# Small VectorE operations on SBUF made on GpSimd and ScalarE, a planner that knows the shared SBUF port, and TensorE listed in two lanes

## The chip, the cores and the metric

The kernel runs on one core of a Trainium2 chip. Its engines work from queues of their own and wait for one another by semaphores: TensorE (PE, with its weight loads PEld) multiplies matrices into PSUM, VectorE (DVE) and ScalarE (ACT) compute on SBUF and PSUM, GpSimd (POOL) computes on SBUF, and SyncE (SP) issues nearly all DMA transfers. The metric is the device time of one execution in microseconds (us), lower is better; the time of a kernel is the median of its runs.

## The reference

```python
def reference(A_x, A_wqkv, A_wo, B_x, B_w1, B_w3, B_w2):
    x = A_x                                   # (1, 2048, 512)
    xn = _layernorm(x, axis=-1)
    s = _A_ref(xn, A_wqkv, A_wo)              # attention, 32 heads of 16, causal, window 256
    g = _silu(_B_ref(xn, B_w1, B_w3, B_w2))   # (silu(xn w1) * (xn w3)) w2, inner width 1792
    return x + s * g
```

All inputs and the output are float32.

## The kernel before

**Tiles.** The 2048 tokens are cut into four token tiles t of 512, the 32 heads into four groups g of eight, and each group into two halves p. A (t, g, p) is a unit of attention; there are 32, and they run in this order. The kernel keeps float32 accuracy on 16-bit matmuls: every factor is scaled by a power of two and split into a high and a low float16 half, and a product is three matmuls (high by high, high by low, low by high).

**Attention.** For a unit, `pass1` multiplies queries by keys into a scores bank of PSUM (`s`, or `po` in a batch marked X), and VectorE takes each query's masked maximum into `M` (L616). When all eight rows are there, L621 and L622 split the negated maxima into two float16 halves `NM`; TensorE transposes them in the next unit (`finish`, L631), VectorE copies them out (L637) and SyncE sends them through DRAM into two extra rows of the queries `qa`. The extra rows of the keys `KA` hold constant ones, so that `pass2` gets scores with the maximum already subtracted: matmuls with the keys standing (L678), the mask added by VectorE (L685), the exponential by ScalarE (L688), then the product with the values V (L706), whose last column of ones gives the denominator. `normalise` inverts the denominators (L743, with a scale in L744) and multiplies.

**Feed-forward.** For a tile t and a block f of 128 columns, `gate_up` makes two products of 24 matmuls (L937); ScalarE takes the tanh (L948), VectorE the two products (L952, L957), and the result is split by ScalarE and GpSimd (L963, L316). `down` (first tile, and the last blocks of the last tile) multiplies with w2 (L987) and VectorE adds the bank to its sum (L1007); for the other tiles `product` does the same with seven products of half blocks instead of eight (L1040, L1053), whose left and right factors GpSimd sums (L869 to L872, L910 to L913).

**What is special in the first tile.** During t = 0 the weights arrive as float32. Each is measured: sums of squares (`squares`), added over partitions by TensorE beside a row of scores (`powers`, L279), then turned on VectorE into a power of two and its inverse on 128x1 to 128x6 elements (L288 to L294) and into scales (L798 to L800, L849 to L855). With these ScalarE and GpSimd split the weights (L319, L320, L316), and SyncE stores them for the later tiles. The inverse root of layernorm is a chain of twelve steps on 128x4 elements on VectorE (`rstd`, L427 to L437), once for each tile; the centred tokens (L440) are turned by TensorE beside scores (`turn_beside`, L478) and split by two VectorE operations, L487 (high half) and L488 (low half). The tiles 1 and 2 are prepared within t = 0, tile 3 within t = 1.

**What sets the order.** The program is written down as one list: a unit's batches of scores, between them (`spread`) the dense pieces of the feed-forward and projections. TensorE runs it in that order. Matmuls of dense pieces go into two banks `m0` and `m1` by turns, so a new dense bank waits until the one before last has been emptied. The other engines are ordered by `listed`: it plays the list through, with a cost for each instruction (`cost`) and a delay to its reader (`extra`), and takes on each engine, among the instructions that are ready, the one that is due first; due times (`deadlines`) are counted back from TensorE's own clock. In its costs a VectorE operation on four elements takes 84 ns, whatever GpSimd does. The order found is fixed by dependencies without semaphores.

## Time and profile before

| | us |
|---|---|
| median of 3 runs (lowest, highest) | 819.23 (818.41, 819.41) |
| profiled execution, its own time | 821.13 |
| its span, first to last instruction | 819.3 |
| ScalarE busy | 435.3 |
| mean granted TensorE clock | 0.994 |
| VectorE's groups L621 and L622, 32 each | 9.0 and 9.7 |
| VectorE's group L744, 16 | 4.4 |

A row of the profile names the line, the engine, the operation, the tile written and the tiles read, the shapes and the count. After the bar stand the busy us of the group and the mean ns of one, then the engine's idle time just before, and what ended it. In a timeline the first number is the start in us, the second the length; brackets hold the idle time before and what ended it. A busy TensorE is not TensorE at its peak: the ends of matmuls are modelled. The granted clock is 1.00 at full speed.

### The profile page before, as it was taken

How to read it: one execution, taken by the hardware profiler on the slowest of the kernel's cores; microseconds unless marked ns; L12 is line 12 of the kernel's file. 1: busy time of each engine (PE TensorE's matmuls, PEld its weight loads, DVE VectorE, ACT ScalarE, POOL GpSimd, SP SyncE). 2: the span in 40 equal slices, each digit the busy share in tenths (PEclk: the TensorE clock that was granted, in tenths of full speed). 3: DMA queues.
4: the chain of work that ended last, by engine and by line, in shares of the span. 5: the costliest groups of instructions: out<-in, count | busy, mean ns of one | idle time of the engine just before them, and what ended most of it. 6: DMA issues, size and time to landing. Idle time of an engine off the chain costs nothing.

```text
span 819.3 us, 23768 instructions
## 1 busy us (share of the span) xinstructions
PE 797.9 (97%) x9088; PEld 415.8 (51%) x9088; DVE 639.2 (78%) x2044; ACT 435.3 (53%) x659; POOL 358.7 (44%) x556
## 2 busy tenths in 40 slices
PE   8999999699999999999999999999999999999998
PEld 4444444344544554454555555545555555545654
DVE  8898889977897777799778866777878787774535
ACT  6898799555636554443443455534443446544421
POOL 2247646672806433523341752514141456435252
PEclk9999999899999999999999999999999999999999
DMA  9996575268665334545364452426375543224521
GB/s 284 284 296 185 164 215 169 75 197 204 176 179 136 117 103 121 152 144 154 106 189 133 125 142 69 140 72 172 112 185 152 159 146 113 56 90 149 172 65 55
DMA packets 112835, 121.99 MB, mean 149 GB/s; under 512 B 18448, under 2 KB 77008, under 8 KB 112720
## 3 DMA queue, kind: packets, MB, share of 16 engines
q1 hardware_dynamic: 112432, 119.94, 51.2%
q8 instruction: 71, 1.16, 0.6%
q10 hardware_dynamic: 288, 0.52, 0.2%
q14 instruction: 44, 0.36, 0.1%
HBM read 83.76 MB, written 32.37 MB: 142 GB/s over the span
## 4 chain that ended last, share of the span: by engine, by line
PE 83%; DVE 12%; issue 2%; DMA 1%; ACT 1%; DVEq 0%; SPq 0%; ACTq 0%
PE m L937 32%; PE m L1040 9%; PE m L550 9%; PE po L706 8%; PE s L678 5%; PE m L1118 5%; PE m L520 5%; PE m L987 4%; DVE junk L616 3%; PE s L604 3%; DVE s L685 2%; PE po L604 2%; DVE st L422 1%; DMA qa<-dQ 1%; DVE slot L957 1%
## 5 line engine op out<-in xcount | busy, mean ns | idle before, releaser
L688 ACT ACTIVATE pt<-s,es 128x1024 f32<-128x1024 f32 x152 | 167.7, 1113 | 198.0 <-DVE s L685 193.3
L937 PE MATMUL m<-XH,slot 128*128 128x512 f16 x896 | 267.4, 380 | 1.0 <-DVE slot L952 0.8
L316 POOL TENSOR_TENSOR slot<-slot,slot 128x256 f16<-128x256 f32 (+1 forms) x222 | 148.6, 696 | 152.4 <-ACT slot L320 66.6
L937 PEld LDWEIGHTS <-slot 128*128 128x128 f16 x1344 | 124.5, 98 | 152.6 <-issue 12.3
L937 PE MATMUL m<-XL,slot 128*128 128x512 f16 x448 | 169.8, 379 | 0.0
L685 DVE TENSOR_TENSOR s<-s,MK 128x256 f32<-128x256 f32 (+2 forms) x280 | 120.7, 437 | 50.4 <-PE s L678 41.9
L616 DVE CUSTOM_DVE_ANT_0 junk<-s,MW 128x320 bf16<-128x320 f32 x276 | 134.5, 487 | 28.0 <-PE s L604 18.6
L906 POOL TENSOR_TENSOR slot<-slot,slot 128x256 f16<-128x256 f32 x133 | 87.9, 685 | 46.4 <-ACT slot L902 46.3
L1040 PE MATMUL m<-slot,slot 128*128 128x256 f16 x798 | 96.4, 276 | 2.0 <-DVE s L685 1.8
L616 DVE CUSTOM_DVE_ANT_0 junk<-po,MW 128x320 bf16<-128x320 f32 x172 | 84.0, 488 | 10.0
L1040 PEld LDWEIGHTS <-slot 128*128 128x128 f16 x798 | 76.9, 99 | 20.4 <-issue 4.5
L706 PE MATMUL po<-pt,V 64*32 64x320 f32 (+4 forms) x2880 | 78.2, 345 | 0.0
L706 PEld LDWEIGHTS po<-pt,V 64*32 64x32 f32 x2880 | 51.9, 106 | 23.8 <-PE s L604 4.0
L910 POOL TENSOR_TENSOR slot<-slot,slot 128x256 f32<-128x256 f32 x19 | 14.2, 747 | 102.8 <-DVE slot L957 96.5
L678 PE MATMUL s<-qa,KA 50*64 50x320 f16 (+3 forms) x1472 | 58.2, 259 | 1.0 <-ACT pt L688 1.0
L987 PE MATMUL m<-slot,slot 128*128 128x512 f16 x216 | 51.6, 386 | 7.0 <-DVE slot L1007 4.7
L952 DVE SCALAR_TENSOR_TENSOR slot<-slot,m 128x512 f32<-128x512 f32 x56 | 38.3, 683 | 24.0 <-ACT slot L948 23.8
L678 PEld LDWEIGHTS <-KA 50*64 50x64 f16 x1472 | 30.2, 105 | 50.9 <-issue 36.3
L716 ACT COPY os<-po 128x512 f32<-128x512 f32 x32 | 18.7, 585 | 70.2 <-PE po L706 70.2
L948 ACT ACTIVATE slot<-m,sgs 128x512 f32<-128x512 f32 x56 | 38.3, 684 | 32.2 <-PE m L937 31.3
L957 DVE SCALAR_TENSOR_TENSOR slot<-m,slot 128x512 f32<-128x512 f32 x56 | 38.5, 687 | 15.9 <-PE m L937 15.5
L604 PE MATMUL s<-KA,qa 48*64 48x320 f16 (+2 forms) x648 | 45.5, 295 | 1.9 <-DVE M L616 0.7
(170 smaller groups left out, 1137.1 us busy)
## 6 DMA issues: line engine op xcount, KB each, us to landing
slot<-dW SPq DMA_DIRECT2D x88, 256.0 KB
slot<-dR SPq DMA_DIRECT2D x56, 256.0 KB
slot<-in_B_w_dram SPq DMA_DIRECT2D x42, 256.0 KB
dW<-slot SPq DMA_DIRECT2D x32, 256.0 KB
slot<-in_A_x_dram SPq DMA_DIRECT2D x30, 256.0 KB
KA<-dK SPq DMA_DIRECT2D x24, 288.0 KB
dR<-slot SPq DMA_DIRECT2D x49, 128.0 KB
qa<-dQ SPq DMA_DIRECT2D x32, 192.0 KB
```

The costliest lines, as they stand in the source:

```text
L316: op(out[:, c], a[:, c], b[:, c])
L550: nc.tensor.matmul(cell["pp"], a[:, k, c, :], b[:, c, :], start=(c, i) == parts[0][0], stop=(c, i) == parts[-1][-1])
L604: nc.tensor.matmul(s[64 * c:64 * c + 64, r, :n], qa[rows, 2 * p + a, ii * P + 64 * c:ii * P + 64 * c + 64], ka[rows, 2 * p + a, e - n:e], ...
L616: nc.vector.tensor_tensor_reduce(out=junk[:, :n], in0=s[:, r, :n], in1=mask, scale=1.0, scalar=NEG, op0=ALU.add, op1=ALU.max, accum_out=M[ ...
L678: nc.tensor.matmul(s[64 * h:64 * h + 64, r, o:o + 64 * n], ka[rows, 2 * p + a, 64 * (m + 4):64 * (m + 5)], qa[rows, 2 * p + a, 64 * (m + k ...
L685: nc.vector.tensor_add(v, v, MK[:, kind, of:of + n, :].unsqueeze(1).to_broadcast([P, 2 * len(which), n, 64]))
L688: nc.scalar.activation(pt, s, AF.Exp, scale=es)
L706: nc.tensor.matmul(cell["po"][32 * i:32 * i + 32, h, 64 * (m + k):64 * (m + k + n)], V[64 * h:64 * h + 64, (4 * t + m // 2) % VB, hd * VW: ...
L906: nc.gpsimd.tensor_sub(made[:, D + c.start:D + c.stop], raw[:, c], made[:, c])
L937: nc.tensor.matmul(cell[k], w[:, (a * NC + c) * P:(a * NC + c + 1) * P], b[:, c, :], start=c == 0 and i == 0, stop=c == NC - 1 and i == 2)
L987: nc.tensor.matmul(ps, hh[:, a * TW + b * P:a * TW + (b + 1) * P], w[:, c * D:(c + 1) * D], start=f == f0 and i == 0, stop=f == f1 - 1 and ...
L1040: nc.tensor.matmul(ps[:, blk, :], l[:, a * D + q:a * D + q + 128], r[:, 256 * c:256 * c + 256], start=f == f0 and x == 0, stop=f == f1 - 2 ...
```

## The change

It has four parts.

1. *Operations moved.* The roots of tiles 1 to 3 (`rstd_beside`), the powers of two with their inverses, and the scales made from them go to GpSimd once the opening is over (`aside`); the inverse is now an integer subtraction of exponents instead of a reciprocal. The maxima are taken with a scale of 1/ONE and without the sign, which is put into the ones of the keys instead, so that their split is one ScalarE copy and one GpSimd subtraction. The high half of a turn is copied by ScalarE (L487's copy). The scale of the denominators (L744) is dropped: it is in the values' column of ones, which ScalarE now writes. The shift that makes a power of two now reads PSUM.
2. *The planner's costs.* New costs per engine, with terms for operands in SBUF and for a second input; delays by engine, and one between dependent instructions of the same engine; `shares` names the instructions that use the port which VectorE and GpSimd share, and such instructions are played one after the other.
3. *TensorE in two lanes.* The matmuls are cut into blocks of up to six that are dense (bank `m`) or not. Each lane keeps its own order, but where the next block in the list is not ready, the other lane's next may go first, if it is at most 8 us ahead. The play is run four times, each time from the order found before.
4. *Order fixed for TensorE too*, by the same dependencies, and the kernel is no longer traced under a fixed TensorE schedule.

```diff
-                    nc.vector.scalar_tensor_tensor(al, s[:, 1, WIN:WIN + n], 2.08, al, op0=ALU.mult, op1=ALU.add)
-            nc.vector.tensor_scalar(p2, al, 2.0**63, None, op0=ALU.mult)
-            nc.vector.reciprocal(inv, p2)
+                    nc.vector.scalar_tensor_tensor(s[:, 1, WIN:WIN + n], s[:, 1, WIN:WIN + n], 2.08, al, op0=ALU.mult, op1=ALU.add)
+            op = nc.vector if s is None else nc.gpsimd
+            nc.vector.tensor_scalar(al.bitcast(I32), (al if s is None else s[:, 1, WIN:WIN + n]).bitcast(I32), 24, 23,
+                                    op0=ALU.logical_shift_right, op1=ALU.logical_shift_left)
+            op.tensor_scalar(p2, al, 2.0**63, None, op0=ALU.mult)
+            if s is None:
+                nc.vector.reciprocal(inv, p2)
+            else:
+                op.tensor_scalar(inv.bitcast(I32), p2.bitcast(I32), -1.0, float(254 << 23), op0=ALU.mult, op1=ALU.add)
...
+    def aside():
+        return nc.gpsimd if started else nc.vector
...
+        def rstd_beside(b0, b1):
+            op = nc.gpsimd
+            ve = lnpool.tile([P, b1 - b0], F32, name="ve")
+            op.tensor_scalar(ve, mv[:, b0:b1, 1], 1e-5, None, op0=ALU.add)
+            r0 = lnpool.tile([P, b1 - b0], F32, name="r0")
+            op.tensor_scalar(r0.bitcast(I32), ve.bitcast(I32), -0.5, float(0x5F3759DF), op0=ALU.mult, op1=ALU.add)
+            sq = lnpool.tile([P, b1 - b0], F32, name="sq")
+            for i in range(3):
+                op.tensor_mul(sq, r0, r0)
+                op.tensor_mul(sq, sq, ve)
+                op.tensor_scalar(sq, sq, -0.5, 1.5, op0=ALU.mult, op1=ALU.add)
+                op.tensor_mul(r0, r0, sq)
+            op.tensor_scalar(rs[:, b0:b1], r0, XS, None, op0=ALU.mult)
...
-                    nc.vector.tensor_copy(hi, pt)
+                    nc.scalar.copy(hi, pt)
                     nc.vector.tensor_sub(lo, pt, hi)
...
-                nc.vector.tensor_scalar(nm[:, 0, :], Mf, -1.0 / ONE, None, op0=ALU.mult)
-                nc.vector.scalar_tensor_tensor(nm[:, 1, :], Mf, -1.0 / ONE, nm[:, 0, :], op0=ALU.mult, op1=ALU.subtract)
+                nc.scalar.copy(nm[:, 0, :], Mf)
+                nc.gpsimd.tensor_sub(nm[:, 1, :], Mf, nm[:, 0, :])
...
             nc.vector.reciprocal(dr, dr)
-            nc.vector.tensor_scalar(dr, dr, sc["o"], None, op0=ALU.mult)
...
-            nc.vector.tensor_scalar(pi, pi, WS, None, op0=ALU.mult)
-            nc.vector.tensor_scalar(sg_scale[:, ff], pp[:, 0, :], 0.5 / (WS * XS), None, op0=ALU.mult)
-            nc.vector.tensor_mul(p13[:, ff], pp[:, 0, :], pp[:, 1, :])
+            aside().tensor_scalar(pi, pi, WS, None, op0=ALU.mult)
+            aside().tensor_scalar(sg_scale[:, ff], pp[:, 0, :], 0.5 / (WS * XS), None, op0=ALU.mult)
+            aside().tensor_mul(p13[:, ff], pp[:, 0, :], pp[:, 1, :])
...
         if i.engine == ENGINE.Activation:
-            return 130 + 0.98 * n + 50 * (len(i.outs) > 1)
+            return 30 + (0 if psum else 30) + 0.9 * n + 95 * scales + 30 * more
         if i.engine == ENGINE.DVE:
-            return 80 + 1.05 * n + (6 * n if kind == "InstReciprocal" else 0) + 45 * (len(i.outs) > 1)
-        return 40 + 2.6 * n
+            return max(160, (185 if inputs > 1 or len(i.outs[0].ap) < 2 or i.outs[0].ap[-1][1] < n else 95) + 0.98 * n + 55 * (scales == 1) + (5 * n if kind == "InstReciprocal" else 0)) - 80
+        if n <= 64:
+            return 130 + (14 if kind == "InstTensorScalarPtr" else 2.1) * n
+        return 2.68 * n - 42 if inputs else 0.85 * n
+
+    def shares(i):
+        if i.engine == ENGINE.Pool:
+            return type(i).__name__ != "InstMemset"
...
+        if len(big) > 1:
+            return sum(big) > 1
+        return all(big) and getattr(i.outs[0].bass_ap.tensor, "space", None) != PSUM
...
+        def next_block():
+            able = sorted((lane[h] for lane, h in zip(lanes, heads) if h < len(lane)), key=lambda b: when_of[b])
...
+            f = free[ENGINE.PE]
+            first = met[able[0]] if not open_[able[0]] else None
+            if len(able) > 1 and (first is None or first > f + GAIN):
+                o = able[1]
+                if not open_[o] and when_of[o] - when_of[able[0]] < LEADING and (
+                        first is None or max(f, met[o]) + GAIN < first):
+                    return max(f, met[o]), o
+            return None if first is None else (max(f, first), able[0])
...
             start[k] = s
-            free[e] = s + took[k]
+            if shared[k]:
+                s = max(s, port - 140)
+                port = s + took[k] + 80
...
-ROUNDS, SHIFT = 3, False
+PIECE, GAIN, LEADING, FOLLOW = 6, 300, 8000, 0.0
+ROUNDS = 4
```

**VectorE, where the down products of the second group of blocks empty their first bank** (tile 0; `mv`, `rs`, `ve`, `r`, `sq` belong to the root of tile 2, `dsc` is the scale of the sum, `m_2573` the bank). Before:

```order
L427 TENSOR_SCALAR ve<-mv 128x4
L430 TENSOR_SCALAR r_2849<-ve 128x4
L431 TENSOR_SCALAR r_2849<-r_2849 128x4
L434 TENSOR_TENSOR sq<-r_2849 128x4
L435 SCALAR_TENSOR_TENSOR sq<-sq,ve 128x4
L436 SCALAR_TENSOR_TENSOR r_2849<-sq,r_2849 128x4
L437 TENSOR_SCALAR rs<-r_2849 128x4
L440 TENSOR_SCALAR slot_2469<-slot_2469,mv,rs 128x512
L440 TENSOR_SCALAR slot_2471<-slot_2471,mv,rs 128x512
L1007 SCALAR_TENSOR_TENSOR slot_1423<-m_2573,dsc,slot_1423 128x512
```

(L434 to L436 stand there three times.) And now (line 1035 is the old 1007, 510 the old 488, 638 the old 616, 430 and 431 the statistics):

```order
L638 ISA junk,M<-po,MW 128x320
L638 ISA M 128x1
L510 TENSOR_TENSOR XL<-po,XH 128x2x128
L510 TENSOR_TENSOR XL<-s,XH 128x2x128
L431 BN_AGGR mv<-st 128x2
L1035 SCALAR_TENSOR_TENSOR slot_1413<-m_2565,dsc,slot_1413 128x512
L430 BN_STATS st<-slot_2465 128x6
L431 BN_AGGR mv<-st 128x2
L430 BN_STATS st<-slot_2467 128x6
```

The root and the centring no longer stand ahead of the sum that empties the bank; part of that tile's statistics now comes behind it.

**GpSimd, a root among the splits of weights** (tile 0, the root of tile 1; L324 is the old L316, L900 a sum of down weights). These rows were not there; the splits were next to each other:

```order
L436 TENSOR_SCALAR ve<-mv 128x4
L900 TENSOR_TENSOR slot_1576<-slot_816,slot_1575 128x256
L438 TENSOR_SCALAR r_1960<-ve 128x4
L827 TENSOR_TENSOR p_155<-pp 128x2
L441 TENSOR_TENSOR sq<-r_1960 128x4
L442 TENSOR_TENSOR sq<-sq,ve 128x4
L443 TENSOR_SCALAR sq<-sq 128x4
L444 TENSOR_TENSOR r_1960<-r_1960,sq 128x4
L324 TENSOR_TENSOR slot_1327<-slot_806,slot_1327 128x256
L441 TENSOR_TENSOR sq<-r_1960 128x4
L324 TENSOR_TENSOR slot_1327<-slot_806,slot_1327 128x256
```

Root steps and splits now take turns on GpSimd.

**TensorE, the first bank of those down products** (`slot_2428` and `slot_2459` are down weights, `slot_2072` and `slot_2267` the split hidden blocks). Before, the third six of the bank follow the second:

```order
L987 LDWEIGHTS slot_2072
L987 MATMUL m_2573<-slot_2428,slot_2072 128x512
L987 LDWEIGHTS slot_2267
L987 MATMUL m_2573<-slot_2459,slot_2267 128x512
L987 LDWEIGHTS slot_2267
```

And now a batch of scores, with two halves of a turn, comes between:

```order
L1015 LDWEIGHTS slot_2064
L1015 MATMUL m_2565<-slot_2420,slot_2064 128x512
L700 LDWEIGHTS KA_139
L700 MATMUL s<-qa,KA_139 64x320
L700 LDWEIGHTS KA_139
```

There are some eight such places, all but one in the first tile (in the one later place six matmuls of L937 move between two halves of a row of scores); the rest of TensorE's list is as it was.

At the start, five matmuls that only keep TensorE busy (L1327) now stand ahead of the sum of squares of the first weights (L274) instead of behind it; VectorE's powers of two for these weights are worked in between the steps of the first root, and ScalarE casts the weights ahead of the four copies of the turned tokens instead of between them.

191 lines of the change are left out of this document (137 added, 54 removed).

## The prediction

> **What bounds the kernel now.** I read the page first, then the busy time of each engine by stretches, then TensorE's own waits, then the timeline of the one long wait.
>
> ```profile
> span 819.3 us, 23768 instructions
> PE 797.9 (97%) x9088; PEld 415.8 (51%) x9088; DVE 639.2 (78%) x2044; ACT 435.3 (53%) x659; POOL 358.7 (44%) x556
> ```
>
> TensorE sets the time: it is idle for 819.3 - 797.9 = 21.4 us, and the change leaves its 9088 matmuls as they are. Whatever the change wins must come out of those 21.4 us, or out of time at half clock. The stretches show where they lie (columns after the length: busy us and instructions of each engine, then granted clock).
>
> ```profile
> core 0: us, PE busy (x) PEld busy (x) DVE busy (x) ACT busy (x) POOL busy (x), PEclk, DMA share, GB/s
> 60.00:85.00 25.00, 24.20 (x250) 11.25 (x252) 21.53 (x80) 22.37 (x41) 19.69 (x30) 1.00 0.60 181
> 85.00:110.00 25.00, 23.23 (x246) 10.99 (x239) 23.11 (x83) 19.20 (x34) 13.94 (x22) 1.00 0.67 201
> 110.00:135.00 25.00, 24.69 (x308) 12.05 (x305) 20.82 (x87) 23.28 (x43) 9.95 (x16) 1.00 0.62 181
> 135.00:165.00 30.00, 22.96 (x250) 10.60 (x248) 27.90 (x81) 19.22 (x33) 22.32 (x35) 0.89 0.33 99
> 165.00:400.00 235.00, 233.48 (x2773) 119.14 (x2773) 189.45 (x621) 118.44 (x165) 104.04 (x155) 1.00 0.55 153
> 400.00:745.00 345.00, 344.49 (x4315) 186.99 (x4314) 269.06 (x830) 161.23 (x216) 141.56 (x209) 1.00 0.44 126
> 745.00:755.00 10.00, 8.21 (x56) 4.79 (x55) 3.71 (x8) 4.54 (x6) 5.72 (x9) 0.83 0.64 192
> 755.00:819.30 64.30, 60.59 (x574) 34.37 (x571) 32.92 (x66) 17.26 (x23) 22.96 (x32) 1.00 0.33 100
> ```
>
> From 165 to 745 us TensorE idles 1.52 + 0.51 = 2.0 us out of 580: nothing to win there, only something to lose. From 60 to 165 it idles 0.80 + 1.77 + 0.31 + 7.04 = 9.9 us, and in the last of these stretches the clock is 0.89 while VectorE is busy for 27.9 of 30 us. So the change has to act on the first token tile, where the weights are measured and split. TensorE's waits, longest first (us in total, times, longest):
>
> ```profile
> PE m L987 <- DVE slot L1007: 4.7, 1, 4.7
> PE m L987 <- POOL slot L316: 2.0, 5, 0.6
> PE m L1040 <- DVE s L685: 1.8, 1, 1.8
> PE s L678 <- ACT pt L688: 1.0, 1, 1.0
> PE m L937 <- DVE slot L952: 0.8, 2, 0.5
> PE m L520 <- DVE slot L563: 0.8, 1, 0.8
> PE s L604 <- DVE M L616: 0.7, 1, 0.7
> PE s L604 <- ACT pt L688: 0.4, 1, 0.4
> PEld L1040 <- DMA slot<-dR: 2.1, 1, 2.1
> ```
>
> **The long wait and its cause.** The timeline around it, with the same instruction 62 us earlier:
>
> ```profile
> 89.32 0.16 DVE L436 SCALAR_TENSOR_TENSOR r<-sq,r 128x4 f32<-128x4 f32 x1
> 91.23 1.44 POOL L316 TENSOR_TENSOR slot<-slot,slot 128x256 f16<-128x256 f32 x2 [2.77 <-ACT slot L320]
> 149.74 1.46 PE L987 MATMUL m<-slot,slot 128*128 128x512 f16 x6
> 150.70 3.17 POOL L316 TENSOR_TENSOR slot<-slot,slot 128x256 f16<-128x256 f32 x5
> 151.42 0.59 DVE L436 SCALAR_TENSOR_TENSOR r<-sq,r 128x4 f32<-128x4 f32 x1
> 155.05 0.75 DVE L1007 SCALAR_TENSOR_TENSOR slot<-m,dsc,slot 128x512 f32<-128x512 f32 x1
> 155.85 2.72 PE L987 MATMUL m<-slot,slot 128*128 128x512 f16 x6 [4.66 <-DVE slot L1007]
> ```
>
> At 89.32 GpSimd has been idle (it starts again at 91.23, after 2.77 us) and a root step on 128x4 elements takes 0.16 us. At 151.42 GpSimd runs without a break and the same step takes 0.59, nearly one GpSimd operation. The VectorE operations whose operands all lie in SBUF wait for GpSimd; the root of the third tile, which nobody needs yet, stands ahead of L1007, and TensorE waits 4.66 us for L1007 to empty its bank. Then six matmuls take 2.72 us where they took 1.46: 1.26 us of half clock.
>
> The Trainium skill, SBUF — State Buffer, section Who interferes with whom, says that a VectorE instruction with two SBUF inputs, or in a two-port mode, and a GpSimd instruction lock each other out of a shared port for a whole instruction. The pair 0.16 and 0.59 agrees.
>
> **Term 1: the root and the small scales leave VectorE.** In 135 to 165 us:
>
> ```profile
> L436 DVE SCALAR_TENSOR_TENSOR r<-sq,r 128x4 f32<-128x4 f32 x3 | 1.8, 612 | 0.1
> L435 DVE SCALAR_TENSOR_TENSOR sq<-sq,ve 128x4 f32<-128x4 f32 x3 | 1.8, 588 | 0.1
> L434 DVE TENSOR_TENSOR sq<-r 128x4 f32<-128x4 f32 x3 | 1.4, 469 | 0.1
> L487 DVE CAST XH<-po 128x256 f16<-128x256 f32 x3 | 1.3, 420 | 0.0
> ```
>
> These four groups alone are 6.3 of VectorE's 27.9 us and all go. In the new VectorE list no root step stands ahead of the bank's release; four statistics and two halves of a turn do, and a whole block of 18 matmuls covers them (six take 1.46 us with the last one's tail, so 18 take some 4). I count the wait and its clock as gone: 4.66 + 1.26 = 5.9 us. If half the cover were missing, 3 us would be left.
>
> **Term 2: the smaller waits of the same kind**, L952 0.8, L616 0.7 and L688 1.0 + 0.4 (its mask add waits on VectorE): 2.9 us. They follow other roots and powers of two on VectorE. I take 2.3, between 0 and 2.9.
>
> **Term 3: after 165 us.** L563's 0.8 stands behind maxima, not behind a root, but VectorE loses work there too. I take 0.4, with 2.0 (all idle time) as the bound. L1040's wait is no VectorE wait: the weight load of the same product waits 2.1 us for a DMA of dR, whose slot and place in SyncE's list stay nearly as they were. I leave it, half clock (0.83) included.
>
> **Term 4: what GpSimd gets.** No row of before has a GpSimd operation on so few elements. The bounds and the rows nearest in size:
>
> ```profile
> L316 POOL TENSOR_TENSOR slot<-slot,slot 128x256 f16<-128x256 f32 x156 | 101.3, 678 | 102.8 <-ACT slot L320 66.6 <-ACT slot L963 33.5 <-ACT slot L877 1.6
> L221 POOL TENSOR_SCALAR_AFFINE_SELECT MK<-MK 64x64 bf16<-64x64 bf16 x4 | 0.8, 234 | 0.0
> L227 POOL MEMSET NM<- 128x64 f16 x3 | 0.4, 152 | 0.0
> L902 ACT CAST slot<-slot 128x256 f16<-128x256 f32 x19 | 7.6, 402 | 5.2 <-DVE slot L957 5.2
> ```
>
> A memset of 64 columns takes 0.15, a select of 64 columns 0.23, a two-input operation on 256 columns 0.68. One to sixteen columns lie nearest the 64: I take 0.23 each, between 0.15 and 0.68. Of 132 moved operations 27 fall into 135 to 165 us (15 of the root, two measurements of 5, two maxima): 27 x 0.23 = 6.2 us on top of 22.3, in a stretch that shrinks from 30 to 24 us. GpSimd is then over-full by 4.5 us there. Part can slide: the sums of the down weights and the normalising products are not urgent, and TensorE's list now has a scores batch and two turns between the second and the third six of the down matmuls that waited 2.0 us for L316. I take 0.9 us lost, between -2.0 (those waits gone) and +4.5.
>
> **Term 5: ScalarE's share.** 24 halves of a turn at about 0.40 (the 128x256 cast) are 9.6 us, 32 copies of maxima at 0.2 to 0.4 some 10, on an engine 53% busy. Each first half was followed by its second on VectorE; now that waits for ScalarE, behind an exponential at worst, while the scores bank stays held. The maxima chain gets one engine longer. The tightest place is the last unit:
>
> ```profile
> 741.51 0.18 DVE L622 SCALAR_TENSOR_TENSOR NM<-M,NM 128x16 f16<-128x16 f32 x1
> 742.79 0.22 PE L631 MATMUL s<-identh,NM 64*64 64x64 f16 x2
> ```
>
> 742.79 - 741.69 = 1.1 us of slack, enough for one more hand-over when ScalarE and GpSimd are free. I take 0.2 lost, between 0 and 3.
>
> **Term 6: the start.**
>
> ```profile
> 9.68 0.17 DVE L437 TENSOR_SCALAR rs<-r 128x4 f32<-128x4 f32 x1
> 9.98 0.19 PE L274 MATMUL s<-sb,onesb 128*128 128x1 bf16 x2 [1.53 <-DVE sb L259]
> 14.88 1.02 PE L550 MATMUL s<-XH,whi 128*128 128x512 f16 x4 [0.46 <-ACT XH L459]
> ```
>
> The first tile's root stays on VectorE, but the first weights' scale is now worked in between its steps, and one of those steps waits for L274, which now stands behind five more warm-up matmuls. The root's end at 9.85 slips to about 11; the first projection hangs on the last ScalarE copy, and ScalarE now casts the weights ahead of those copies instead of between them. Between -0.3 and +1.2; I take 0.4.
>
> **The sum.** -5.9 - 2.3 - 0.4 + 0.9 + 0.2 + 0.4 = -7.1 us. The profiled execution took 821.13 us (span 819.3 and 1.8 around it), so 814.0 for such a one; the median of the runs, 819.23, lies 1.9 below it, which gives **812.1 us**.
>
> **Rivals.**
>
> *All waits go.* If term 4 falls on its good side and the new lists also catch the rest, the waits listed above but L1040's (4.7 + 2.0 + 1.0 + 0.8 + 0.8 + 0.7 + 0.4 = 10.4) and the clock's 1.26 vanish: 807.5. For it: the planner's new costs and second lane move work away from exactly these places. Against it: GpSimd's load.
>
> *GpSimd becomes the bound* in the first tile. At 0.68 us for each small operation, 27 cost 18.4 us and the stretch needs 22.3 + 18.4 = 40.7 us: 10.7 more than before, less terms 2 and 3: 827. The point from which it decides is (30 - 22.3)/27 = 0.29 us an operation, where the stretch is as long as it was. The select's 0.23 speaks against it, the dependence of each root step on the one before for it.
>
> *Nothing is won.* The lock is only turned round: where VectorE waited for GpSimd, the small steps now queue on GpSimd behind 0.68 us each, and their consumers (weight splits, maxima) are late instead. If half of term 1 and all of terms 2 and 3 come back as waits for GpSimd, 3.0 us are left of the gain; 2.0 us of new waits after 165 us and 0.3 at the start leave 0.7: 818.5. Against it: the maxima and mask adds that fill VectorE (L616, L685) have a scores bank, not SBUF, as their large input, so they do not wait for GpSimd now and need not then.
> The Trainium skill, Perfetto Trace Analysis, section Optimizing Scalar/DVE Operations, warns that moving operations between GpSimd and VectorE "might not help", since they share an SBUF read port. By that rule this rival is the outcome.
>
> *Scores banks held longer.* 24 turns and 32 maxima with 0.1 us each passed on to TensorE would cost 5.6 us; with half of the 7.1 lost too that is 821.3. The slack of units before the last speaks against it.
>
> **How the numbers follow.** Forecast 0.54 (809 to 816); all waits go 0.20; nothing won 0.13; GpSimd the bound 0.08; banks 0.05. The range to the other cases is 805 to 820. A measurement of this kernel tells 0.2%, 1.6 us, from no change. Faster by more: 0.54 + 0.20 + 0.05 of the third case = 0.79. Within: 0.08. Slower: 0.13.
>
> **What would show it.** Right: no wait on L1035 (the old L1007) of over 1 us and no half clock near 150 us; root steps on GpSimd at 0.2 to 0.3 us; VectorE under 600 us busy, its remaining small steps at 0.16; TensorE's idle time near 14 us, still with a DMA wait near 740 us. Wrong: small GpSimd steps of 0.5 us or more, TensorE waiting for L316's successor in several pieces between 130 and 165 us, or new waits between 165 and 745 us that sum to more than 3 us, where before has 2.0.

## The result, and the profile after

| | us |
|---|---|
| before, median of 10 runs (lowest, highest) | 819.72 (818.41, 821.44) |
| after, median of 10 runs (lowest, highest) | 816.24 (814.42, 818.09) |
| ratio, 95% interval | 0.9954 (0.9941 to 0.9967) |
| profiled execution of after, its own time and span | 818.09, 816.3 |

The change won 3.5 us where 7.1 were forecast: faster by more than 0.2%, by half of the size. The ten executions of after differ by 3.7 us, and the mean granted clock of TensorE goes with them: 0.993 at 818.1 us, 0.998 at 814.4 to 815.3. The profiled execution is the slowest of the ten, 1.9 us above the median, and so holds more half clock than most. In the changed kernel the old L1007 is L1035, L316 is L324, L987 is L1015, L688 is L710, L440 is L462, L1093 is L1121, L1118 is L1146 and L1040 is L1068. The page of after begins:

```profile
span 816.3 us, 23767 instructions
PE 798.9 (98%) x9088; PEld 417.8 (51%) x9088; DVE 591.5 (72%) x1846; ACT 445.6 (55%) x716; POOL 382.7 (47%) x678
```

VectorE lost 47.7 us of work, ScalarE got 10.3 and GpSimd 24.0. TensorE idles 17.4 us (816.3 - 798.9) instead of 21.4. Its busy time by stretches, with the columns shown before:

```profile
60.00:135.00 75.00, 73.81 (x803) 35.00 (x802) 54.90 (x203) 65.45 (x123) 54.97 (x118) 1.00 0.69 211
135.00:165.00 30.00, 28.18 (x340) 14.02 (x338) 20.15 (x70) 23.85 (x45) 27.87 (x54) 1.00 0.36 107
...
755.00:816.30 61.30, 54.50 (x480) 29.40 (x457) 26.77 (x52) 13.98 (x19) 20.63 (x30) 0.96 0.26 79
```

From 60 to 135 us TensorE now idles 1.2 us (before, in three stretches, 2.9), from 135 to 165 us 1.8 (before 7.0), and the clock there is 1.00 (before 0.89). From 165 to 745 us it idles 4.1 us instead of 2.0, but 2.1 of these are the old wait for a DMA of dR, which in after comes at about 741 to 743 us and so ahead of 745. Behind 755 us it idles 6.8 us where it idled 3.7, at a clock of 0.96 instead of 1.00. Its longest waits in after:

```profile
PE m L1146 <- DVE slot L1035: 3.0, 1, 3.0
PE m L478 <- DVE slot L462: 2.1, 1, 2.1
PE m L1068 <- DMA slot<-dR: 2.1, 1, 2.1
...
PE m L1015 <- POOL slot L324: 0.5, 1, 0.5
```

The first two are new, and neither lies in the first token tile's feed-forward: one is the start, one the tail. How far after is ahead of before is read from the same matmul in both traces, here the transposition of the last maxima (before: 742.79, shown with the prediction) and the first matmul of the last output products (before, then two rows of after):

```profile
805.03 7.93 PE L1118 MATMUL m<-slot,slot 128*128 128x512 f16 x36
```

```profile
734.57 0.22 PE L653 MATMUL s<-identh,NM 64*64 64x64 f16 x2
800.21 9.63 PE L1146 MATMUL m<-slot,slot 128*128 128x512 f16 x36 [2.96 <-DVE slot L1035]
```

At 742.79 after is 8.2 us ahead, at 805.03 only 4.8, and the 36 matmuls then take 1.7 us longer, at half clock behind the wait; the spans differ by 3.0. So in these two traces more was won up to 742.79 us than was forecast for the whole, and more than half of it was given back.

**The first tile.** The timeline of after where the long wait was:

```profile
145.15 6.65 PE L1015 MATMUL m<-slot,slot 128*128 128x512 f16 x30
148.47 0.72 DVE L1035 SCALAR_TENSOR_TENSOR slot<-m,dsc,slot 128x512 f32<-128x512 f32 x1
157.80 0.20 POOL L441 TENSOR_TENSOR sq<-r 128x4 f32<-128x4 f32 x1
...
168.95 0.21 POOL L441 TENSOR_TENSOR sq<-r 128x4 f32<-128x4 f32 x1
```

Thirty matmuls run in one go, the bank is released at 148.47, and the root of tile 2 is spread over GpSimd from 156 to 172 us, a step at a time between weight halves. GpSimd's groups in after (busy us and mean ns behind the bar):

```profile
L324 POOL TENSOR_TENSOR slot<-slot,slot 128x256 f16<-128x256 f32 x156 | 102.2, 678 | 84.9 <-ACT slot L328 47.6 <-ACT slot L991 33.0 <-ACT slot L905 2.9
L644 POOL TENSOR_TENSOR NM<-M,NM 128x16 f16<-128x16 f32 x32 | 7.2, 224 | 80.1 <-ACT NM L643 80.0
L298 POOL TENSOR_SCALAR pi<-pp 128x4 int32<-128x4 int32 x7 | 1.8, 264 | 0.6
L441 POOL TENSOR_TENSOR sq<-r 128x4 f32<-128x4 f32 x9 | 1.8, 198 | 0.2
```

A small operation costs GpSimd 0.19 to 0.28 us over all its groups; its large ones take 678 ns, as before.

**The start.** Six rows of after between the root and the first projection:

```profile
8.77 0.16 DVE L456 TENSOR_TENSOR sq<-r 128x4 f32<-128x4 f32 x1
10.48 0.19 PE L274 MATMUL s<-sb,onesb 128*128 128x1 bf16 x2
10.72 0.16 DVE L285 TENSOR_SCALAR al<-s 128x1 f32<-128x1 f32 x1 [1.79 <-PE s L274]
11.87 0.17 DVE L459 TENSOR_SCALAR rs<-r 128x4 f32<-128x4 f32 x1
12.77 1.73 PE L478 MATMUL m<-identf,slot 128*128 128x128 f32 x8 [2.10 <-DVE slot L462]
17.07 1.03 PE L572 MATMUL s<-XH,whi 128*128 128x512 f16 x4
```

VectorE's root stands still for 1.79 us, because a step of the first weights' power of two, placed in its middle, waits for L274, which stands behind 31 warm-up matmuls instead of 26. TensorE then waits 2.10 us for the centred tokens, and the turns behind that wait run at half clock (granted clock 0.50 from 13 to 16 us; eight turns in 1.73 us, before 1.04). The first projection starts at 17.07 instead of 14.88: 2.2 us lost.

**The tail.** Before, and then after, where the last sums of the down products meet the gates of the last tile (L1093, now L1121):

```profile
794.67 10.52 PE L987 MATMUL m<-slot,slot 128*128 128x512 f16 x48
802.70 0.73 DVE L1093 SCALAR_TENSOR_TENSOR slot<-slot,slot 128x512 f32<-128x512 f32 x1 [1.77 <-ACT slot L1092]
803.35 0.86 DVE L1007 SCALAR_TENSOR_TENSOR slot<-m,dsc,slot 128x256 f32<-128x256 f32 x2
```

```profile
786.72 10.52 PE L1015 MATMUL m<-slot,slot 128*128 128x512 f16 x48
794.95 1.40 POOL L324 TENSOR_TENSOR on<-on,rb 128x256 f32<-128x256 f32 x2 [5.31 <-DMA rb<-de]
796.38 0.62 ACT L776 CAST slot<-on 128x512 f16<-128x512 f32 x1 [8.12 <-POOL on L324]
796.91 1.14 ACT L1120 ACTIVATE slot<-slot 128x512 f32<-128x512 f32 x2
797.56 1.80 DVE L1121 SCALAR_TENSOR_TENSOR slot<-slot,slot 128x512 f32<-128x512 f32 x2 [4.58 <-ACT slot L1120]
799.29 1.65 DVE L1035 SCALAR_TENSOR_TENSOR slot<-m,dsc,slot 128x256 f32<-128x256 f32 x4
```

In after two gates stand ahead of the third bank's sum in VectorE's list, where before had one. They wait for ScalarE's L1120, which stands behind the cast L776, which waits for GpSimd, which waits for the DMA of rb. VectorE is idle for 4.58 us, in the later part with a full bank to empty (in the run `tail`, below, that sum starts at 794.85), and TensorE waits 2.96 us for that bank. Before has the same chain, but only one gate ahead of the sum, and the sum came in time.

### The profile page after: what moved, and what is told of

It reads as the page before. It is cut to its first block, busy times and chain, and to the rows that moved or that the text cites. A ratio compares the mean times of both kernels' runs of the same rounds, so it can differ in the third digit from the quotient of the medians.

```text
span 816.3 us, 23767 instructions
## 1 busy us (share of the span) xinstructions
PE 798.9 (98%) x9088; PEld 417.8 (51%) x9088; DVE 591.5 (72%) x1846; ACT 445.6 (55%) x716; POOL 382.7 (47%) x678
## 4 chain that ended last, share of the span: by engine, by line
PE 85%; DVE 5%; ACT 2%; POOL 2%; DMA 2%; issue 2%; SPq 1%; POOLq 0%; DVEq 0%; ACTq 0%
PE m L965 31%; PE m L1068 10%; PE m L572 9%; PE po L728 9%; PE s L700 5%; PE m L1146 5%; PE m L542 5%; PE m L1015 4%; PE s L626 3%; DVE junk L638 2%; POOL slot L324 2%; PE po L626 1%; PE m L1355 1%; DVE s L707 1%; ACT pt L710 1%
## 5 line engine op out<-in xcount | busy, mean ns | idle before, releaser
L710 ACT ACTIVATE pt<-s,es 128x1024 f32<-128x1024 f32 x152 | 167.6, 1112 | 146.3 <-DVE s L707 141.8
L324 POOL TENSOR_TENSOR slot<-slot,slot 128x256 f16<-128x256 f32 (+1 forms) x222 | 148.8, 694 | 123.3 <-ACT slot L328 47.6
L1068 PE MATMUL m<-slot,slot 128*128 128x256 f16 x798 | 96.2, 276 | 2.3 <-DMA slot<-dR 2.1
L1068 PEld LDWEIGHTS <-slot 128*128 128x128 f16 x798 | 76.9, 99 | 20.5 <-issue 4.3
L1015 PE MATMUL m<-slot,slot 128*128 128x512 f16 x216 | 49.3, 379 | 1.1 <-DVE slot L980 0.6
L1146 PE MATMUL m<-slot,slot 128*128 128x512 f16 x180 | 43.4, 391 | 3.0 <-DVE slot L1035 3.0
L930 ACT CAST slot<-slot 128x256 f16<-128x256 f32 (+1 forms) x76 | 40.8, 564 | 8.3 <-DVE slot L985 7.7
```

The source lines that it names most:

```text
L324: op(out[:, c], a[:, c], b[:, c])
L710: nc.scalar.activation(pt, s, AF.Exp, scale=es)
L1015: nc.tensor.matmul(ps, hh[:, a * TW + b * P:a * TW + (b + 1) * P], w[:, c * D:(c + 1) * D], start=f == f0 and i == 0, stop=f == f1 - 1 and ...
L1068: nc.tensor.matmul(ps[:, blk, :], l[:, a * D + q:a * D + q + 128], r[:, 256 * c:256 * c + 256], start=f == f0 and x == 0, stop=f == f1 - 2 ...
L1146: nc.tensor.matmul(ps, O[t, g][:, a, tb], w[g], start=g == 0 and i == 0, stop=g == NG - 1 and i == 2)
```

## The experiments

All ratios are to the kernel before, run on the same chip in the same session. A ratio need not be the quotient of the two medians (for tail the medians give 0.9924, the ratio is 0.9911), so small differences between two versions are given both ways.

| run | what | median us | ratio (95% interval) |
|---|---|---|---|
| tail | after, gates of the last tile behind the last sums | 813.27 | 0.9911 (0.9894 to 0.9927) |
| start | after, planned anew with one more rule at the start | 824.36 | 1.0048 (1.0033 to 1.0063) |
| ops_only | operations of after, planner of before | 824.63 | 1.0050 (1.0035 to 1.0066) |
| plan_only | operations of before, planner of after | 823.99 | 1.0055 (1.0039 to 1.0071) |
| before_hoist | before, the bank's sum ahead of the root | 820.72 | 1.0012 (1.0003 to 1.0022) |
| root_late | before, the root put off on VectorE | 812.65 | 0.9916 (0.9896 to 0.9936) |
| root_pool | before, the root on GpSimd, spread | 813.00 | 0.9917 (0.9896 to 0.9937) |
| root_early | before, the root on GpSimd, in one go | 815.37 | 0.9940 (0.9920 to 0.9959) |
| a_after | after, a planner's margin 1% larger | 822.19 | 1.0031 (1.0021 to 1.0042) |
| b_after | before, the same margin 1% larger | 830.93 | 1.0136 (1.0120 to 1.0151) |
| start_tail | after, start and tail mended in the lists | 811.16 | 0.9895 (0.9881 to 0.9908) |
| back_dve | start_tail, two moved groups back on VectorE | 811.64 | 0.9905 (0.9888 to 0.9922) |

### tail: what the gates cost

```diff
+    for first, then in PAIRS:
+        for k in EDGES[then]:
+            before[number[k]].update(number[j] for j in EDGES[first])
...
+PAIRS = [("sum", "gate"), ]
```

"sum" are the last tile's L1035, "gate" its L1121 in the second `gated` branch; the planner gets a dependency from each sum to each gate. The lists that it finds differ from those of after in six rows, all VectorE's and at the tail: the two gates and the sums change places, and two rows behind them.

> The changed kernel with one rule more for the planner: the gates of the last token tile (VectorE, from two SBUF operands) stand behind the last sums of its down products. Only VectorE's list changes, in six rows at the end. Theory: the changed kernel's gain of about 8 us, which its matmuls still have at 790 us, is given back because two gates wait on VectorE for ScalarE, GpSimd and the DMA of rb ahead of the third bank's sum; then TensorE's wait of 2.96 us for that sum and the half clock behind it (about 1.8 us) go, and the time is 816.2 - 4.8 = 811.4 us (ratio 0.990). Rival: the gates are needed anyway and the stall only moves to the banks of the output product that they scale, so at most 1.5 us are won: 814.7 or more (ratio above 0.993).

Measured: 813.27 us, 0.43% below after by the ratios; the spans of the profiled executions differ by 4.6 us (816.3 and 811.7). TensorE's rows of this run (L1150 is after's L1146):

```profile
786.87 10.52 PE L1015 MATMUL m<-slot,slot 128*128 128x512 f16 x48
797.23 8.00 PE L1150 MATMUL m<-slot,slot 128*128 128x512 f16 x36
```

No wait is left between the two, and the 36 matmuls take 8.00 us instead of 9.63: 2.98 and 1.63 us, the 4.6 us between the spans. The medians differ by 3.0, and the intervals of the two ratios leave 2 to 5 us. The rival (at most 1.5 us) falls. The medians hold little more than the wait: executions with the same mean granted clock, after's three at 0.996 (816.2 us on average) and tail's four (813.4), lie 2.9 us apart, and only two of after's ten have the 0.993 of its profiled one. So the theory was right on the wait, and took the half clock of one execution for all.

### ops_only and plan_only: each half alone

The tile program of after with `arrange`, `listed` and the constants of before, and the reverse.

> The changed kernel's operations under the planner of before (one lane, old costs, TensorE in program order). Theory: the gain in the first tile comes from the operations that left VectorE: no wait for the bank's release near 150 us, start and end as before, and so more gained than with the new planner: 819.7 - 8 = 811 to 814 us (ratio 0.990 to 0.993). Rival: the new planner made the first tile's gain by keeping GpSimd and VectorE apart and by swapping blocks; under the old one the small steps queue on GpSimd and the time is 818 to 821 us (ratio 0.998 to 1.002).

> The operations of before under the new planner (two lanes, new costs, the shared port). Theory: VectorE keeps its roots, but the planner now knows what they cost beside GpSimd and moves them off the bank's release, so that half of the first tile's gain (4 to 5 us) is there, and the start and the tail give back what they gave back in the changed kernel or about it (up to 6.8): 817 to 822 us (ratio 0.997 to 1.003). Rival: the planner alone makes the whole gain and the operations nothing: 816.2 or less (ratio 0.9954 or less).

Measured: 824.63 and 823.99 us. Each half alone is slower than before, by 0.5%, and both together are faster. Neither theory on ops_only foresaw that: its rival named the right side, but the wait at the bank's release is gone in it; it lost its time at other places (a wait of 2.3 us for an exponential, 2.3 for GpSimd, and small ones). plan_only missed its theory's range by 2 us. In it the root of tile 2 is still VectorE's and there is no wait at the bank's release either: the new planner had put the root's first step at 158.7 us, behind two sums. Moving the operations and moving the root in the list are two ways to get rid of that wait. The losses of the start and the tail are in plan_only too (waits of 2.2 us for L440 at the start and 2.3 for L1007 ahead of L1118) and not in ops_only, so they come with the new planner and not with the operations. Why both lists are worse elsewhere is a question for the next three runs.

### start: one rule, everything planned anew

```diff
+PAIRS = [("root", "power"), ]
```

> The changed kernel with one other rule for the planner: the first weights' power of two stands behind the first root on VectorE. The planner's play then differs in small ways later too. Theory: the first root ends near 10 us instead of 12.04, VectorE has no wait of 1.8 us inside it, the first projection starts at 15.0 instead of 17.07 us, and the 2 us last to the end: 814.2 us (ratio 0.9930). Rival: the first tile has slack behind the start (weights that arrive by DMA, measurements), the matmuls after 165 us stand where they stood, and the time stays 816.2 (ratio 0.9954).

Measured: 824.36 us, 8 us more than after, which neither expected. The first root ended at 10.15 us and the first projection came at 15.98, so 1.1 of the 2.2 us came back at the start. But the play went another way from there on: from 17 to 165 us TensorE idles 7.2 us (after: 3.3), from 165 to 790 us 9.9 (after: 4.1), in small waits but for one of 3.7. A rule given to the planner is no clean experiment unless its lists differ in one place alone, as those of tail do. From here on the lists are edited after they have been found, or the perturbation itself is what is tested.

### a_after and b_after: how far a neighbouring order lies

```diff
-AFTER_DMA, AFTER, CLOSE = 4000, 1000, 2000
+AFTER_DMA, AFTER, CLOSE = 4000, 1010, 2000
```

> The changed kernel with one of its planner's margins raised by a hundredth (1000 to 1010 ns, the spare time that a reader on another engine is given). TensorE's list stays word for word, the lists of VectorE, ScalarE, SyncE and GpSimd change in some 280 rows each. Theory: the planner's order is one draw from many that lie several microseconds apart, so that the time moves by more than 2 us from 816.2 (ratio below 0.993 or above 0.998). Rival: what the change won is the work of its rules, not of the draw, and the time stays within 1 us of 816.2 (ratio 0.994 to 0.9967).

> The kernel before with the same margin raised by the same hundredth. Theory: the kernel before is such a draw too, and a poor one in the first tile, where a bank's release stands behind a root: with other places its time moves by more than 2 us from 819.5 (ratio below 0.9975 or above 1.0025). Rival: its time stays within 1 us of 819.5 (ratio 0.9988 to 1.0012), and the wait of 4.66 us is still there.

Measured: 822.19 and 830.93 us, 6 and 11 us above the kernels that they were made from. TensorE's list is the same, the operations are the same. Some waits of a_after, then of b_after:

```profile
PE s L700 <- DVE al L292: 2.5, 1, 2.5
PE s L626 <- ACT pt L710: 2.2, 5, 0.9
```

```profile
PE m L987 <- DVE slot L1007: 4.6, 1, 4.6
PE m L520 <- DVE slot L563: 2.7, 1, 2.7
```

The orders found by two settings 1% apart lie further from one another than before and after do. Apart from tail, whose new play changed six rows, five kernels were planned anew, and all five are slower than the kernels whose planner or operations they share. The theory holds in both cases; it calls before a poor draw, and there it is wrong as far as these few draws go: before is a good one with one bad place.

### before_hoist, root_late, root_pool, root_early: the long wait by itself

In before's finished list for VectorE one row or one group is moved; root_pool and root_early also make tile 2's root on GpSimd, with `rstd_beside`. No other row of any list moves. The diff shows before_hoist (L1007 of the waiting bank), root_late (the root, which has 13 steps in before's list, and the 4 centrings behind it), root_pool (15 steps, one by one) and root_early (the same in one go).

```diff
+    of_dve.remove(down)
+    of_dve.insert(of_dve.index(root), down)
...
+    for moved, at in ((root, 2379), ([2138], 2431), ([2150], 2473), ([2180], 2524), ([2192], 2568)):
+        for k in moved:
+            of_dve.remove(k)
+        i = of_dve.index(at) + 1
+        of_dve[i:i] = moved
...
+    for n, k in enumerate(root):
+        of_pool.insert(at + 2 * n, k)
...
+    of_pool[at:at] = root
```

> The kernel before, with one row of VectorE's list moved: the sum that empties the first bank of the second group of down products (tile 0) goes ahead of the root of tile 2 instead of behind it and two of the centring operations. No operation changes its engine. Theory: the 4.66 us wait and the 1.26 us of half clock near 150 us are a matter of this one place in the list, and the time falls by 5.9 us: 813.6 us (ratio 0.9928). Rival: VectorE is full there (27.9 of 30 us), the wait returns at the next bank or scores bank, and 1 to 3 us are won: 816.5 to 818.5 (ratio 0.9963 to 0.9988).

Measured: 820.72 us, nothing won. Six rows of it:

```profile
147.38 0.72 DVE L1007 SCALAR_TENSOR_TENSOR slot<-m,dsc,slot 128x512 f32<-128x512 f32 x1
148.55 4.06 PE L987 MATMUL m<-slot,slot 128*128 128x512 f16 x18
154.43 0.17 DVE L437 TENSOR_SCALAR rs<-r 128x4 f32<-128x4 f32 x1
156.50 0.42 DVE L685 TENSOR_TENSOR s<-s,MK 128x256 f32<-128x256 f32 x1
157.62 1.11 ACT L688 ACTIVATE pt<-s,es 128x1024 f32<-128x1024 f32 x1 [7.14 <-DVE s L685]
158.79 0.48 PE L604 MATMUL s<-KA,qa 48*64 48x320 f16 x4 [6.18 <-ACT pt L688]
```

The bank is released at 147.38 and the 18 matmuls run through. Then TensorE waits 6.18 us for the next scores bank: its mask add L685 and so its exponential stand behind the same root. The wait was never the bank's own; it is the root's, and whatever stands behind the root inherits it. The theory failed and the rival had the place right (the next scores bank), though even its 1 to 3 us were not won.

> The kernel before, with the root of tile 2 and its four centrings put off in VectorE's list, from 147 us to the stretch behind 183 us, where the trace shows GpSimd idle and VectorE half busy; tile 2's first turn needs them at 210 us. Nothing changes its engine, no other list changes. Theory: the root is the whole cause of the wait near 150 us, for the bank and for the scores bank behind it, and the time falls by 4.66 + 1.26 = 5.9 us: 813.7 us (ratio 0.9928). Rival: the new place costs VectorE what the old one did, or the stretch near 150 us is bound by VectorE's or GpSimd's sum of work, and at most 2 us are won: 817.5 or more (ratio 0.9975 or more).

> The kernel before, with the root of tile 2 alone made on GpSimd (its 15 steps one by one between GpSimd's own operations from 162 us on, as the changed kernel has them) and the four centrings at the places behind 183 us. All other rows of all lists stay. Theory: the same 5.9 us as from putting the root off, since GpSimd's 15 steps take some 0.2 us each and nobody waits for them: 813.7 us (ratio 0.9928). Rival: the 15 x 0.2 = 3 us delay GpSimd's weight halves in its busiest stretch, and TensorE's wait for them (2.0 us before) grows by up to 3: 815 to 817 us (ratio 0.9945 to 0.997).

> As the run before, but GpSimd makes the 15 steps in one go at 147.7 us, in front of its weight halves, where VectorE had them. Theory: GpSimd pays 15 steps of 0.2 to 0.25 us with their gaps, some 3.5 us, ahead of weight halves for which TensorE waited already; it waits for them up to 3.5 us more, and 2.4 to 5.9 us are won: 813.7 to 817 us (ratio 0.9928 to 0.997). Rival: steps of one engine that depend on one another cost GpSimd 0.6 us or more, as they cost VectorE beside it, 9 us in all, and nothing is won: 820 us or more (ratio 1.0005 or more).

Measured: 812.65, 813.00 and 815.37 us. In root_late TensorE's only wait from 135 to 190 us is the old one for GpSimd, and the root's steps take 0.16 us at their new place; in root_pool GpSimd takes 0.20 for one. A wait and a step of root_late, then two groups of root_pool:

```profile
PE m L987 <- POOL slot L316: 2.0, 5, 0.6
```

```profile
175.58 0.16 DVE L434 TENSOR_TENSOR sq<-r 128x4 f32<-128x4 f32 x1
```

```profile
L316 POOL TENSOR_TENSOR slot<-slot,slot 128x256 f16<-128x256 f32 x28 | 18.2, 672 | 9.7 <-ACT slot L977 9.6
L436 POOL TENSOR_TENSOR r<-r,sq 128x4 f32<-128x4 f32 x3 | 0.6, 203 | 0.0
```

Taking the root, with its centrings, out of that stretch wins 6.6 to 6.9 us, by whichever engine it is made; the share of the centrings was not tried by itself. In one go ahead of GpSimd's weight halves it is 2.4 us slower than spread in the medians (by the ratios 0.23%, with intervals that overlap). The time lies inside the theory's range, but not for its reason: TensorE's wait for L316 stays 2.0 us. Up to 165 us root_early has gained as much over before as root_pool (7.4 us each, counted from 140 us on). It then loses 1.2 us between 170 and 172 us, behind a VectorE cast of four elements that lasts until GpSimd has finished a series of its operations (root_early, then root_pool):

```profile
166.13 2.73 DVE L855 CAST sb<-ssq 128x4 bf16<-128x4 f32 x1
165.57 0.88 DVE L855 CAST sb<-ssq 128x4 bf16<-128x4 f32 x1
```

The one row group of root_late, with no operation moved to another engine, is faster than the whole change.

The Trainium skill, Perfetto Trace Analysis, section Optimizing Scalar/DVE Operations, says that moving operations between GpSimd and VectorE might not help. Here moving the root did help: 813.00 us against 819.59 for the kernel before in the same session. But a later place on VectorE gave as much (812.65), so the gain is one of place and not of engine.

### start_tail: both losses mended, nothing planned anew

The rule of tail, and three edits of the finished lists:

```diff
+    place(ENGINE.PE, sums, best_order[ENGINE.PE][27])
+    place(ENGINE.DVE, chain, named(ENGINE.DVE, 40, "slot")[3], True)
+    place(ENGINE.Activation, halves[:1], turns[1])
+    place(ENGINE.Activation, halves[1:], turns[3], True)
```

`sums` are the two L274, `chain` the six steps from L285 to L408, `turns` the copies L481, `halves` the weight casts L318; `place` puts them ahead of an instruction, or behind it with True.

> The changed kernel with the rule for the tail (gates behind the last sums) and, at the start, three places of the finished lists set back to those of before, with nothing else replanned: the first two-column sum of powers ahead of the five warm-up matmuls on TensorE, the first weights' power of two behind the first root and the centring on VectorE, and the first turn's copy ahead of the weight casts on ScalarE. Theory: the first projection starts at 14.9 us instead of 17.07, and the 2.1 us last: 813.3 - 2.1 = 811.2 us (ratio 0.9886). Rival: the first tile takes the 2 us up in waits for weights and measurements before 165 us, and the time stays that of the kernel with the rule for the tail alone, 813.3 us (ratio 0.9911).

Measured: 811.16 us. Three rows of it:

```profile
9.31 0.19 PE L274 MATMUL s<-sb,onesb 128*128 128x1 bf16 x2
9.93 0.17 DVE L459 TENSOR_SCALAR rs<-r 128x4 f32<-128x4 f32 x1
15.13 1.02 PE L572 MATMUL s<-XH,whi 128*128 128x512 f16 x4 [0.46 <-ACT XH L481]
```

The first projection is 1.9 us earlier than in after (1.8 earlier than in tail), and the median is 2.1 below that of tail; by the ratios it is 1.3 us, and the intervals of the two overlap. The number is the theory's, the way to it only half. TensorE's list is that of tail but for L274, and the same matmuls show how the lead goes: 1.8 us at the first projection, 1.0 from 30 to 200 us, 1.2 at 740. So the first tile takes up about half of it, as the rival said of the whole. The other 0.9 us comes behind the wait for dR near 742 us, where tail's granted clock is 0.82 to 0.84 and start_tail's is 1.00. No edit touches that place; whether the earlier start has to do with it is not shown. This version is faster than both kernels, by 1.05% than before.

### back_dve: what the other moved operations bring

In start_tail's lists the 24 high halves of the turns and the 64 operations on the maxima are VectorE's again.

```diff
-                    nc.scalar.copy(hi, pt)
+                    nc.vector.tensor_copy(hi, pt)
...
-                nc.scalar.copy(nm[:, 0, :], Mf)
-                nc.gpsimd.tensor_sub(nm[:, 1, :], Mf, nm[:, 0, :])
+                nc.vector.tensor_copy(nm[:, 0, :], Mf)
+                nc.vector.tensor_sub(nm[:, 1, :], Mf, nm[:, 0, :])
```

> The kernel with the tail and the start mended (811.2 us), with two of the changed kernel's groups of moved operations put back on VectorE in otherwise unchanged lists: the 24 high halves of the turns (from ScalarE, each directly ahead of its subtraction) and the 32 splits of the maxima (64 operations, from ScalarE and GpSimd, directly behind the last maximum). Roots, powers and scales stay on GpSimd. Theory: outside the roots and powers the moves bought nothing, since VectorE has slack of 20 to 30% in every stretch and one engine less in the chain of the maxima saves a hand-over: 811.2 give or take 1.5 us (ratio 0.9875 to 0.991). Rival: VectorE is what TensorE waits for in the first tile, and 24 x 0.42 + 64 x 0.17 = 21 us more on it cost at least 3 us: 814 or more (ratio 0.993 or more).

Measured: 811.64 us (ratio between 0.9888 and 0.9922), not to be told from 811.16; the rival's 0.993 lies outside. In these lists the 88 operations may stand on either side.

## Why the prediction was right in its main term and wrong in its sum

The forecast of 812.1 us was missed by 4.1 us: the measured gain is half of the forecast one. The step that failed is the sum, which has no term for the tail of the kernel; there the new order of VectorE cost 5.2 us in the trace and 3.0 in the medians.

| term | forecast | measured |
|---|---|---|
| 1, the root's wait and its half clock | -5.9 | -6.6 and -6.9 (root_pool, root_late) |
| 2, 3 and 4, other waits, GpSimd's price | -1.8 | some -3.5 (10.4 us won from the first projection to 742.79, less 6.9), which includes what the first tile takes up of the start's loss |
| 5, ScalarE's share | +0.2 | nothing that can be told (back_dve) |
| 6, the start | +0.4 | +2.2 at the first projection; of the 1.8 that start_tail takes back there, 1.0 to 1.2 last |
| the tail | no term | 3.4 + 1.8 = +5.2 in the trace, 3.0 in the medians (tail) |
| sum | -7.1 | -3.0 in the profiled executions, -3.5 in the medians |

**Term 1 was right in its cause and near in its size.** The root was the cause; that it held up one bank was too narrow, as before_hoist shows: "no root step stands ahead of the bank's release" would not have been enough had the root still stood ahead of L685. The half clock was counted for six matmuls only (1.26 us). Before's stretches show it for longer:

```profile
156.00:159.00 3.00, 2.63 (x10) 0.77 (x12) 2.95 (x13) 1.22 (x2) 0.00 (x0) 0.50 0.05 20
159.00:162.00 3.00, 3.00 (x89) 2.20 (x91) 2.91 (x7) 2.57 (x5) 1.39 (x2) 0.68 0.01 3
```

3 x 0.50 + 3 x 0.32 = 2.5 us, an upper value since TensorE also idled. 4.66 + 2.5 is 7.1, near the 6.9 of root_late.

**Term 4 was mis-sized to the cautious side.** The estimate of 0.23 us an operation was right (0.19 to 0.28). But GpSimd's late weight halves did not add 0.9 us: the wait for L316, 2.0 us, is 0.5 in after. It stays 2.0 in root_late and root_pool, so it is other parts of the change (the new lists, the lane of TensorE or the other moved operations) that removed it; which of them was not tried. The rival in which GpSimd becomes the bound is out, and so is the one in which the lock is only turned round: its new waits for GpSimd did not come, and the gain was lost elsewhere.

**Term 6 failed in its size at the first projection.** The step "The root's end at 9.85 slips to about 11" took the order right and left the pace of the warm-up matmuls out. At first they follow one another 0.43 us apart, then 0.21. In before's trace the faster pace comes at 4.0 us, in after's at 6.1; so L274, behind five more of them, came at 10.48, and the root ended at 12.04. With the pace of before's trace five matmuls would have taken 0.21 us less each, and the root would have ended near 11 as forecast (an estimate from these figures). The moment differs between executions of the same list (5.7 us in before_hoist, 6.6 in root_late), so that part is no effect of the change. TensorE's wait then brought half clock of its own. What lasts of the loss, 1.0 to 1.2 us by start_tail, lies inside the term's range of -0.3 to +1.2.

**The sum failed by a term that it lacked.** The prediction looked for gains where before has waits, and read the new lists there. At the tail (755 us to the end) TensorE has no wait in before, so the sum has no term for it, and no reason is given why it could only stay as it was. Two rows in another order cost more there than term 1's error and term 6's together. That the errors have both signs is luck: had terms 1 to 4 come in these traces just as forecast (-7.7), the losses at the start and the tail (+7.4) would have left next to nothing. Of what the prediction named as signs, most came as written: no wait over 1 us for L1035 near 150 us, no half clock there, GpSimd's root steps at 0.20, VectorE at 591.5 us, the wait for dR of 2.1 us still there. TensorE's idle time was to be near 14 us and is 17.4, and most of the difference is the wait of 3.0 at the tail. One sign of being wrong, more than 3 us idle between 165 and 745 us, is there in number (4.1), but 2.1 of it are the old wait for dR at an earlier time.

**What stays open.** Whether the change would win under lists of equal quality can't be said from these runs. Orders found by neighbouring settings differ by 6 to 11 us, and the 3.5 us measured are one pair of orders; that after came out below before at all is in part luck of the draw. What is shown is where this pair differs: start, root, tail. The powers and scales on GpSimd, and the two lanes by themselves, were not tried in fixed lists.

## What to carry to other kernels

When a change replans the order of a whole kernel, read the new lists everywhere, and first where the old kernel had no wait: a stall that is new can't be seen in the old profile. A single operation ahead of a bank's release is not cured by lifting the release over it; move the slow group out of the stretch, and check whether a later place on the same engine does as well as another engine. Test a part of such a change in fixed lists, and perturb the planner once to learn how far apart its orders lie before a few tenths of a per cent are put down to an idea. Where a time agrees with a theory, follow the same matmul through both traces to see whether the gain arises where the theory says.

## What the runs showed of the hardware

- Beside a running GpSimd eight of the nine steps L434 to L436 on 128x4 elements took VectorE 0.58 to 0.65 us (before, 148 to 154 us), alone 0.16. One cast of 128x4 elements took 2.73 us beside four GpSimd operations in a row (root_early), in before 0.25. The reverse does not show: GpSimd's step took 0.20 and its 128x256 operation L316 0.68 on average in before, after, root_late, root_pool and start_tail, and root_pool gained as much as root_late.
- A wait of 3.0 and one of 4.7 us on TensorE were followed by half clock that cost 1.6 us (after, tail: 9.63 and 8.00 us for the same 36 matmuls) to 2.5 us (before, 156 to 162 us). In these two places the half clock added about half of the stall's length to its price. It does not follow every such wait: behind waits for dR of 2.1 us (after) and 2.3 us (tail) the granted clock was 0.81 to 0.85, behind one of 2.05 us (start_tail) it stayed 1.00.
